# Scores of two attention pairs in one run each, and block sums spread by DMA instead of by the vector engine

## The chip, the cores and the metric

The kernel runs on one core of a Trainium2 chip. The metric is the device time of one execution in microseconds (us), lower is better. The engines are called PE (matrix), DVE (vector), ACT (scalar), POOL (GpSimd) and SP (SyncE). One more measure is taken from the traces and used below:

- **the middle stretch**: from the start of the second batch's routing logits (tile `lp`, at 67.20 us in the kernel before) to the start of the last group of eight matmuls (660.53 us). It leaves out the start of the program, which varies by a microsecond between executions, and the closing steps.

Ratios are computed as the mean time of one kernel's fast runs over that of the other's of the same rounds, so they are not quite the ratios of the medians that are quoted.

## The reference, cut to what matters

```python
# attention over (batch 4, heads 8, sequence 768, head dim 64): a band of +-15 positions
# plus 24 block summaries (maximum of keys, mean of values, blocks of 32)
scores_l = scale * q @ k.T                    # masked to |i - j| < 16
scores_s = scale * q @ k_sum.T + log(32)
out = softmax([scores_l, scores_s]) @ [v, v_sum]
# then a mixture of 8 experts on all 3072 rows, weighted by P
P = exp(x @ w_gate); 8 times: normalize the rows, then the columns
y = sum_e P[:, e] * (relu(x @ w1[e]) @ w2[e])
```

## The kernel before

Two heads make a *pair*: 16 pairs, four for each of four batches. While pairs are attended to, expert 0 is applied to the batches that are done; so the matrix engine always finds something to do. The order of instructions on every engine comes from a small planner in the program itself: each unit of work is given an engine, a planned cost and what it depends on, and the planner places the one that can start first. **A changed cost or dependency therefore moves other work too**, and each engine executes its work in the order placed, waiting where something is late (in one experiment below PE stood still for 6.6 us behind one late input). What follows are the parts that the change touches (cuts are marked with ...).

```python
    BY_DMA = 12
    X_BY_DMA = 12
    WHOLE = 12          # pairs from this one on: scores of all 6 chunks in one run
...
        def block_out(i):                 # block sums of the values, from PSUM, into chunk 0 of V_e
            ...
            nc.vector.tensor_tensor(out=dst..., in0=vs, in1=own_n..., op=ALU.mult)
            if i >= PB:                   # and from chunk 0 into chunks 1 to 5
                ve = V_e[i % NE]
                nc.vector.tensor_copy(out=ve[0:64, 1:G, :],
                                      in_=ve[0:64, 0:1, :].to_broadcast([64, G - 1, 2 * VD]))
...
        def scores(i):
            sg = at["sg", i, 0] = banks2("sg")                 # the one slot of two PSUM banks
            dst = [[sg[:, j, :] for j in range(2)], None]
            if i >= WHOLE:                                     # and two of the three small banks "a"
                dst[1] = at["sg", i, 1] = [bank("a", "sg1") for _ in range(2)]
            score_mms(i, dst, range(G if i >= WHOLE else HG))
...
        def score_mms(i, dst, chunks):
            for g in chunks:
                for j in range(2):        # the two heads: 64 rows each, two halves of the array
                    o = (g % HG) * LIVE
                    score_mm(i, dst[g // HG][j][:, o:o + LIVE], j, g, 0, LIVE)
...
                U["A", i, h] = add("PE", 0.4, lambda h=h: values(i, h),      # value products
                                   [U["mk", i, h], U["ed", i], U["sx", i, h], U["Vs", i], U["near", i]],
                                   prio, opens=[buf])
```

The softmax here doesn't subtract the row's maximum and nothing guards it: scores larger than these inputs give would overflow.

Of the kernel before, what the change touches and what calls it, by code (L numbers as in the profile page):

```python
# [33 lines left out]
class Plan:  # L34
# [7 lines left out]
    def add(self, eng, cost, fn, deps=(), prio=0.0, opens=(), uses=(), lag=0.0):  # L42
        u = Unit(eng, cost, fn, [d for d in deps if d is not None], prio, list(opens), lag)
        for b in list(opens) + list(uses):
            b.users.append(u)
        if uses and eng != "PE":
            u.prio -= 100.0
        self.units.append(u)
        return u
# [79 lines left out]
def kernel(  # L129
# [10 lines left out]
    nc = tc.nc  # L140

    B, H, S, D = q.shape
    G = S // 128
# [6 lines left out]
    NP = (B * H) // 2  # L150
    PB = H // 2
# [6 lines left out]
    VD = D + 1  # L158
    NEH = 3
    BY_DMA = 12  # L160
    X_BY_DMA = 12
    WHOLE = 12
    FILL = {"v0": 1, "S0": 1, "s0": 2, "s1": 1, "s2": 1}

    const = ctx.enter_context(tc.tile_pool(name="const", bufs=1))
# [56 lines left out]
    NE = 2  # L222
# [3 lines left out]
    with tc.manual_schedule():  # L226
# [12 lines left out]
        kT = [attn.tile([128, S], BF16, name=f"kT{i}") for i in range(NB)]  # L239
# [9 lines left out]
        V_e = [attn.tile([128, G, 2 * VD], BF16, name=f"Ve{i}") for i in range(NE)]  # L249
# [8 lines left out]
        add = plan.add  # L258
# [101 lines left out]
        def block_out(i):  # L360
            vs = at.pop(("vs", i))[0:64, :].rearrange("p (j d) -> p j d", j=2)
            dst = V_s[i][0:64, :] if i < PB else V_e[i % NE][0:64, 0, :]
            nc.vector.tensor_tensor(out=dst.rearrange("p (j x) -> p j x", j=2)[:, :, 0:D], in0=vs,
                                    in1=own_n[:].to_broadcast([64, 2, D]), op=ALU.mult)
            if i >= PB:
                ve = V_e[i % NE]
                nc.vector.tensor_copy(out=ve[0:64, 1:G, :],
                                      in_=ve[0:64, 0:1, :].to_broadcast([64, G - 1, 2 * VD]))


        def near_values(i):

# [9 lines left out]
        def scores(i):  # L382
            sg = at["sg", i, 0] = banks2("sg")
            dst = [[sg[:, j, :] for j in range(2)], None]
            if i >= WHOLE:
                dst[1] = at["sg", i, 1] = [bank("a", "sg1") for _ in range(2)]
            score_mms(i, dst, range(G if i >= WHOLE else HG))

# [232 lines left out]
        def wait_busy(what, i, h, t):  # L621
            for _ in range(FILL.get(what + str(i), 0) if i < PB and not h else 0):
# [6 lines left out]
                          in_=k[0, 0:2].rearrange("j (p g) d -> p j (g d)", g=G))  # L629
        nc.sync.dma_start(out=v_f32.rearrange("p j g d -> p (j g) d"),  # L630
                          in_=v[0, 0:2].rearrange("j (g p) d -> p (j g) d", p=128))
# [227 lines left out]
        U = {}  # L859
        last = [None, None]  # L860
# [20 lines left out]
        def pair_start(i, prio):  # L881
            o = i - NB
            war_k = [U.get(("S", o, 0)), U.get(("S", o, 1)), U.get(("km", o))]
            war_q = war_k[:2] + [U.get(("ss", o, 0)), U.get(("ss", o, 1))]
            ahead = U.get(("S", i - 1, 1 if i > PB else 0))
            if i >= BY_DMA:
                for z in range(2):
                    U["tr", i, z] = add("SP", 1.4, lambda z=z: tr_dma(i, z),
                                        [U["kq"[z], i], U.get(("S", i - 3, 1))] + (war_k, war_q)[z], prio)
                    U["kT", i, z] = add("DMA", 1.7, None, [U["tr", i, z]], prio, lag=2.0)  # L890
            for z in range(0 if i >= BY_DMA else 1 if i < PB else 2):
                buf = Buffer("m" if i < PB else "a")
                U["tr", i, z] = add("PE", 0.5 if i < PB else 0.34, lambda z=z: tr(i, z),
                                    [U["kq"[z], i], U["ident"]] + (war_k, war_q)[z]
                                    + [U["tr", i, 0] if z else ahead], prio, opens=[buf])
                U["kT", i, z] = add({"ACT": 0.8, "DVE": 0.95 if i < PB else 0.56}, 0,
                                    lambda z=z: tr_out(U["kT", i, z].on, i, z), [U["tr", i, z]], prio,
                                    uses=[buf])
            U["ks", i] = add("DVE", 0.95, lambda: key_max(i), [U["kT", i, 0], U.get(("km", o))], prio)
            if i >= PB:  # L900
                U["km", i] = add("DVE", 0.23, lambda: key_max_split(i), [U["ks", i]] + war_q[2:], prio)
            buf = Buffer("a")
            U["vs", i] = add("PE", 0.4, lambda: block_sums(i),
                             [U["v", i]] + ([U.get(("A", i - NE, 1)), U["vc", i % NE]] if i >= PB else []), prio + 0.01, opens=[buf])
            sc = add("DVE", 0.25, lambda: summary_constants(i), [], prio - 1.0) if 0 < i < PB else None
            U["Vs", i] = add("DVE", 0.28 if i < PB else 0.7, lambda: block_out(i), [U["vs", i], sc],
                             prio + 0.01, uses=[buf])

        def pair_half(i, h, prio):
# [34 lines left out]
        def pair_whole(i, prio):  # L944
            U["near", i] = add("SP" if i < BY_DMA else "POOL", 2.4 if i < BY_DMA else 3.0, lambda: near_values(i),
                               [U["v", i], U.get(("A", i - NE, 1)), U["vc", i % NE]], prio, lag=5.0 if i < BY_DMA else 3.5)
            x1 = []
            deps = [U["kT", i, 0], U["kT", i, 1], U.get(("ed", i - 2))]
            bufs = [Buffer("s")] + (2 * [None] if i < WHOLE else [Buffer("a"), Buffer("a")])
            U["S", i, 0] = U["S", i, 1] = add("PE", 0.4 if i < WHOLE else 0.6, lambda: scores(i), deps, prio,  # L950
                                              opens=[x for x in bufs if x is not None])
            U["X", i, 0] = add("ACT", 0.97, lambda: score_exp(i, 0), [U["S", i, 0]], prio, uses=bufs[:1])
            if i < WHOLE:
                buf = Buffer("s")
                U["S", i, 1] = add("PE", 0.4, lambda: scores_1(i), deps, prio, opens=[buf])
                U["X", i, 1] = add("ACT", 0.97, lambda: score_exp(i, 1), [U["S", i, 1], U["X", i, 0]], prio,
                                   uses=[buf])
            else:
                x1 = [add("ACT", 0.53, lambda j=j: score_exp(i, 1, j), [U["S", i, 0], U["X", i, 0]], prio,
                          uses=bufs[1 + j:2 + j]) for j in range(2)]  # L960
                U["X", i, 1] = x1[1]
            for h in range(2):
                U["mk", i, h] = add("DVE", 0.56, lambda h=h: masks(i, h),
                                    [U["X", i, h], *x1[:h], U.get(("A", i - 2, 1))], prio)
            U["ed", i] = add("DVE", 0.78, lambda: edges(i),
                             [U["X", i, 0], U["X", i, 1], U["mk", i, 1], U.get(("A", i - NE, 1)), U["ec", i % NE]], prio)
            buf = Buffer("a")
            U["ss", i, 0] = U["ss", i, 1] = add("PE", 0.22, lambda: summaries_2(i),
                                                [U["km", i], U["kT", i, 1], U.get(("A", i - NE, 1))], prio, opens=[buf])
            for h in range(2):  # L970
                U["sx", i, h] = add("ACT", 0.46, lambda h=h: summary_exp(i, h), [U["ss", i, h]], prio, uses=[buf])
            for h in range(2):
                buf = Buffer("a")
                U["A", i, h] = add("PE", 0.4, lambda h=h: values(i, h),
                                   [U["mk", i, h], U["ed", i], U["sx", i, h], U["Vs", i], U["near", i]],
                                   prio, opens=[buf])
                U["no", i, h] = add("DVE", 0.75, lambda h=h: normalize(i, h),
                                    [U["A", i, h], U.get(("x", i - 2))], prio, uses=[buf])
            if i >= X_BY_DMA and i % PB < PB - 1:
                U["xt", i] = add("SP", 1.5, lambda: x_dma(i), [U["no", i, 0], U["no", i, 1]], prio)  # L980
                U["x", i] = add("DMA", 1.7, None, [U["xt", i]], prio, lag=2.0)
                return
            buf = Buffer("a")
            U["xt", i] = add("PE", 0.35, lambda: to_xT(i), [U["no", i, 0], U["no", i, 1]], prio, opens=[buf])
            U["x", i] = add({"ACT": 0.8, "DVE": 0.55}, 0, lambda: x_out(U["x", i].on, i), [U["xt", i]], prio,
                            uses=[buf])
# [109 lines left out]
        def transposed():  # L1096
# [7 lines left out]
            for j in range(2):  # L1104
                nc.gpsimd.tensor_copy(out=warm[:, 2 + j:3 + j],
                                      in_=ve[64 + 32 * j:96 + 32 * j, G - 2, VD * j:VD * j + 1])

        last[0] = add("POOL", 0.3, transposed, [last[0], U["near", NP - 1]] + [U["kT", NP - 1, z] for z in range(2)]
                      + [U["x", i] for i in range(X_BY_DMA, NP - 1)])
        load("w1n", lambda: load_w1(1), 0.85, 5.0)  # L1110
        load("w2n", lambda: load_w2(1), 0.85, 5.0)
# [209 lines left out]
```

## Time and profile before

| | before |
|---|---|
| median of 6 runs | 666.79 us (666.71 to 667.56) |
| span of the profiled execution | 665.8 us |
| middle stretch, by the trace | 593.33 us |
| closing part, by the trace | 5.26 us |

The page's first part gives each engine's busy time and share of the span; 99% for PE says that it is the bound. A "busy" PE may still lose time between matmuls. That is read from the distance of successive start times in the timeline, compared with what their columns need, and the prediction below does so.

### The profile page before, as it was taken

To read this page: it belongs to the slowest core of one execution; us is meant where nothing else is said; L and a number is where in the kernel's file an instruction comes from. 1 tells how busy PE (TensorE), PEld (TensorE's weight loads), DVE (VectorE), ACT (ScalarE), POOL (GpSimd) and SP (SyncE) were. 2 spreads that over 40 slices of the span, in tenths; PEclk is the share of its full clock that TensorE was granted. 3 is DMA by queue.
4 is the path that set the end of the run, shared out by engine and by line. 5 is a ranking of instruction groups with operands and counts; after the bars stand their busy time and mean duration, and the time that the engine had idled before them with its cause. 6 is when DMAs were issued, how large, how long until landed. Compare 5 with 4: busy or idle time off the path is not lost.

```text
span 665.8 us, 13247 instructions
## 1 busy us (share of the span) xinstructions
PE 658.5 (99%) x5132; PEld 436.2 (66%) x5132; DVE 550.4 (83%) x1034; ACT 411.4 (62%) x769; POOL 198.8 (30%) x257
## 2 busy tenths in 40 slices
PE   9999999999999999999999999999999999999997
PEld 5666666555676666666666666666666666666666
DVE  7799977798989787887789887888778877988776
ACT  6667866556875566556565665656665656556652
POOL 8799722100132222222222222222122213222123
PEclk9999999999999999999999999999999999999999
DMA  9999992700763747473654756373837465334656
GB/s 166 163 142 146 124 107 42 127 0 1 129 118 58 126 74 116 79 127 64 105 96 66 131 80 110 65 127 64 128 64 131 72 100 96 64 64 110 156 135 202
DMA packets 112558, 67.89 MB, mean 102 GB/s; under 512 B 77936, under 2 KB 90480, under 8 KB 112496
## 3 DMA queue, kind: packets, MB, share of 16 engines
q0 software_dynamic: 94816, 57.46, 65.4%
q1 hardware_dynamic: 17152, 9.58, 6.8%
q8 instruction: 40, 0.66, 0.4%
q14 instruction: 22, 0.18, 0.1%
q10 hardware_dynamic: 528, 0.02, 0.0%
HBM read 52.45 MB, written 6.29 MB: 88 GB/s over the span
## 4 chain that ended last, share of the span: by engine, by line
PE 95%; DVE 2%; DMA 1%; POOL 1%; issue 0%; ACT 0%; POOLq 0%; DVEq 0%
PE yps L815 22%; PE pA L764 22%; PE pY L815 17%; PE pQ L764 11%; PE hps L211 6%; PE yps L216 6%; PE pR L764 5%; DMA w<-in_moe_w_dram 1%; PE sg L347 1%; PE tkq L303 1%; PE av L435 1%; PE av L512 1%; PE ss L461 1%; PE vs L357 1%; PE av L441 1%; PE tx L550 1%
## 5 line engine op out<-in xcount | busy, mean ns | idle before, releaser
L815 PEld LDWEIGHTS <-h 128*128 128x128 f16 x2352 | 230.1, 98 | 89.2 <-issue 1.3
L843 POOL DMA_DIRECT2D out_acc<-y x120 | 101.4, 888 | 372.4 <-ACT y L839 95.5
L839 ACT ACTIVATE y<-pY,P_sb 128x256 f32<-128x256 f32 x168 | 79.9, 476 | 126.3 <-PE pY L815 124.8
L830 DVE SCALAR_TENSOR_TENSOR out_acc<-yps,P_sb,out_acc 128x512 f32<-128x512 f32 x128 | 95.3, 745 | 28.0 <-PE yps L815 27.9
L798 DVE TENSOR_TENSOR h<-h 128x1024 f16<-128x1024 f16 x168 | 109.2, 684 | 1.3
L815 PE MATMUL pY<-w,h 128*128 128x256 f16 x672 | 100.3, 273 | 0.6 <-ACT y L839 0.6
L764 PE MATMUL pA<-xT,w 128*128 128x512 f16 x336 | 98.6, 379 | 0.0
L815 PE MATMUL yps<-w2sum,h 128*128 128x256 f16 x672 | 97.9, 273 | 0.0
L815 PE MATMUL yps<-w,h 128*128 128x256 f16 x672 | 93.3, 273 | 0.0
L830 DVE SCALAR_TENSOR_TENSOR out_acc<-pY,P_sb,out_acc 128x512 f32<-128x512 f32 x84 | 62.9, 749 | 29.1 <-PE pY L815 27.5
L764 PEld LDWEIGHTS <-w 128*128 128x128 f16 x672 | 65.8, 98 | 31.3 <-issue 0.2
L764 PEld LDWEIGHTS <-w1sum 128*128 128x128 f16 x504 | 49.3, 98 | 44.7
L786 DVE CUSTOM_DVE_ANT_0 h<-pQ,snap 128x512 f16<-128x512 f32 x84 | 57.7, 686 | 6.5 <-ACT snap L207 3.6
L786 DVE CUSTOM_DVE_ANT_0 h<-pA,snap 128x512 f16<-128x512 f32 x84 | 57.4, 684 | 5.4 <-PE pA L764 5.1
L202 ACT ACTIVATE h<-pA 128x512 f16<-128x512 f32 x84 | 50.7, 603 | 12.1 <-PE pA L764 12.0
L202 ACT ACTIVATE h<-pR 128x512 f16<-128x512 f32 x84 | 50.1, 596 | 8.1 <-PE pR L764 8.1
L207 ACT COPY pR<-pA 128x512 f32<-128x512 f32 x82 | 46.8, 571 | 6.8 <-PE pA L764 5.9
L815 PE MATMUL pY<-w2sum,h 128*128 128x256 f16 x336 | 50.4, 273 | 0.1
L764 PE MATMUL pA<-xsum,w 128*128 128x512 f16 x168 | 50.0, 379 | 0.0
L764 PE MATMUL pQ<-xsum,w1sum 128*128 128x512 f16 x168 | 50.0, 379 | 0.0
L764 PE MATMUL pQ<-xT,w1sum 128*128 128x512 f16 x168 | 50.0, 379 | 0.0
L764 PE MATMUL pA<-xsum,w1sum 128*128 128x512 f16 x168 | 50.0, 379 | 0.0
(150 smaller groups left out, 854.7 us busy)
## 6 DMA issues: line engine op xcount, KB each, us to landing
out_acc<-y POOLq DMA_DIRECT2D x120, 256.0 KB, 3.4
w<-in_moe_w_dram POOLq DMA_DIRECT2D x14, 1024.0 KB, 10.3
out_dram<-out_acc SPq DMA_DIRECT2D x24, 256.0 KB, 2.4
qst<-in_q_dram POOLq DMA_DIRECT2D x32, 96.0 KB, 5.8
vx<-in_v_dram POOLq DMA_DIRECT2D x15, 192.0 KB, 6.9
kst<-in_k_dram POOLq DMA_DIRECT2D x24, 96.0 KB, 6.1
w<-in_moe_w_dram POOLq DMA_DIRECT2D x4, 256.0 KB, 8.6
w<-in_moe_w_dram POOLq DMA_DIRECT2D x2, 512.0 KB, 8.8
```

What stands on the lines that cost most here:

```text
L202: nc.scalar.activation(out=out, in_=in_, func=AF.Relu, bias=0.0, scale=1.0)
L207: (nc.scalar.copy if eng == "ACT" else nc.vector.tensor_copy)(out=out, in_=in_)
L211: nc.tensor.matmul(hp[:, 0:n], lhsT=w1s[e][:, dk, f * 128:(f + 1) * 128], rhs=xT[:, dk, t0:t0 + n], start=(dk == 0), stop=(dk == KD - 1))
L216: nc.tensor.matmul(yp[:, d], lhsT=h[:, f, c * 128:(c + 1) * 128], rhs=w2s[e][:, f, d], start=(f == 0), stop=(f == KF - 1))
L303: nc.tensor.transpose(t[:, g * 128:(g + 1) * 128], st[:, g, :, :].rearrange("p j d -> p (j d)"), ident)
L764: nc.tensor.matmul(dst[:], lhsT=lhsT, rhs=rhs, start=first and k == 0, stop=k == HK - 1, skip_group_check=True)
L786: nc.vector._custom_dve(dve_ops.TENSOR_ADD_SAT, out=ring(e, p, q)[:, q % 2, blk, :], in0=at[src, e, p, q][:], in1=at.pop(("snap", n, e, p, ...
L798: nc.vector.tensor_tensor(out=h[:, :, out_, :], in0=h[:, :, a, :], in1=h[:, :, b, :], op=op)
L815: nc.tensor.matmul(dst[:, d], lhsT=lhsT, rhs=rhs, start=f == 0 and n in (1, 5, 2), stop=f == HF - 1, skip_group_check=True)
L830: nc.vector.scalar_tensor_tensor(out=o, in0=y, scalar=scalar, in1=o, op0=ALU.mult, op1=ALU.add)
L839: nc.scalar.activation(out=at[key][:, d], in_=src, func=AF.Copy, bias=0.0, scale=P_sb[:, t, e:e + 1])
L843: nc.gpsimd.dma_start(out=o, in_=at.pop(("y", e, p, c, key))[:], accum_op=ALU.add)
```

## The change

Its intent: a pair's scores in one run of 12 matmuls instead of two of 6 for two more pairs, and 1.9 us less work for DVE in the fourth batch, by letting DMA copy the block sums into the chunks.

```diff
-    WHOLE = 12
+    SPREAD = 12
+    WHOLE = 10
...
-            if i >= PB:
+            if PB <= i < SPREAD:
                 ve = V_e[i % NE]
                 nc.vector.tensor_copy(out=ve[0:64, 1:G, :], ...)
+        def spread_sums(i):
+            ve = V_e[i % NE]
+            nc.gpsimd.dma_start(
+                out=ve[0:64, 1:G, :], in_=ve[0:64, 0:1, :].to_broadcast([64, G - 1, 2 * VD]))
...
-            U["Vs", i] = add("DVE", 0.28 if i < PB else 0.7, lambda: block_out(i), ...)
+            U["Vs", i] = add("DVE", 0.7 if PB <= i < SPREAD else 0.28, lambda: block_out(i), ...)
...
+            if i >= SPREAD:
+                U["sp", i] = add("POOL", 1.0, lambda: spread_sums(i), [U["Vs", i]], prio, lag=3.5)
...
-                                   [U["mk", i, h], U["ed", i], U["sx", i, h], U["Vs", i], U["near", i]],
+                                   [U["mk", i, h], U["ed", i], U["sx", i, h], U.get(("sp", i), U["Vs", i]), U["near", i]],
...
-        last[0] = add("POOL", 0.3, transposed, [last[0], U["near", NP - 1]] + ...
+        last[0] = add("POOL", 0.3, transposed, [last[0], U["near", NP - 1], U.get(("sp", NP - 1))] + ...
```

More of the change, by code (lines that the diff above doesn't have):

```diff
@@ L905, in pair_start @@
             sc = add("DVE", 0.25, lambda: summary_constants(i), [], prio - 1.0) if 0 < i < PB else None
-            U["Vs", i] = add("DVE", 0.28 if i < PB else 0.7, lambda: block_out(i), [U["vs", i], sc],
+            U["Vs", i] = add("DVE", 0.7 if PB <= i < SPREAD else 0.28, lambda: block_out(i), [U["vs", i], sc],
                              prio + 0.01, uses=[buf])
@@ L1106, in transposed @@
                                       in_=ve[64 + 32 * j:96 + 32 * j, G - 2, VD * j:VD * j + 1])
-        last[0] = add("POOL", 0.3, transposed, [last[0], U["near", NP - 1]] + [U["kT", NP - 1, z] for z in range(2)]
+        last[0] = add("POOL", 0.3, transposed, [last[0], U["near", NP - 1], U.get(("sp", NP - 1))] + [U["kT", NP - 1, z] for z in range(2)]
                       + [U["x", i] for i in range(X_BY_DMA, NP - 1)])
```

## The prediction

> **What bounds the kernel now.** I read the page's first part, then the busy times by stretch, then the timeline where pairs 10 to 15 run. The first says that the matrix engine is the bound:
>
> ```profile
> PE 658.5 (99%) x5132; PEld 436.2 (66%) x5132; DVE 550.4 (83%) x1034; ACT 411.4 (62%) x769; POOL 198.8 (30%) x257
> ```
>
> A busy PE in this view can still lose time inside, so I compared the distance between the starts of successive matmuls with the time their columns need. The timeline gives that need: four 384-column matmuls start 0.65 us before what follows them, 0.163 us each, 2.36 columns a nanosecond. Where the change acts, the stretches read:
>
> ```profile
> 67.00:84.00 17.00, 16.95 (x203) 11.17 (x201) 15.94 (x45) 13.29 (x23) 11.71 (x15) 1.00 2.23 125
> 84.00:115.00 31.00, 31.00 (x302) 18.73 (x301) 24.14 (x68) 22.00 (x42) 8.43 (x18) 1.00 0.72 70
> 121.00:165.00 44.00, 44.00 (x234) 22.94 (x233) 39.98 (x86) 26.14 (x50) 0.00 (x0) 1.00 0.25 42
> 165.00:217.00 52.00, 51.87 (x363) 35.41 (x362) 47.85 (x76) 38.68 (x73) 12.67 (x15) 1.00 0.60 100
> 217.00:600.00 383.00, 383.00 (x2648) 258.93 (x2647) 313.87 (x484) 229.83 (x442) 87.93 (x104) 1.00 0.57 93
> ```
>
> The columns are length, then PE, weight loads, DVE, ACT and POOL busy. The matrix engine is full in all of them, because attention pairs and expert matmuls are interleaved: when a pair waits, an expert block runs. So an operation taken from another engine is worth nothing by itself; only a gap on PE, or less PE work, moves the end. Gaps of over 60 ns between matmuls add up to only about 2 us from 67 to 200 us, and to none from 200 to 600. That caps the gain near 2 us (0.3%).
>
> What are those gaps? Nearly all stand around the score matmuls, which contract over 64 rows and run as two halves of the array:
>
> ```profile
> 68.77 0.81 PE L211 MATMUL hps<-xT,w 128*128 128x384 f16 x4
> 69.52 0.38 PE L347 MATMUL sg<-qT,kT 64*128 64x160 bf16 x6
> 69.83 0.36 PE L435 MATMUL av<-vx,em 128*128 128x65 bf16 x6
> ...
> 93.19 0.81 PE L211 MATMUL hps<-xT,w 128*128 128x384 f16 x4
> 93.93 0.59 PE L347 MATMUL sg<-qT,kT 64*128 64x160 bf16 x12
> 94.45 2.76 PE L216 MATMUL yps<-w,h 128*128 128x512 f16 x12
> ```
>
> The run of 6 is the first half of pair 10. Four 384-column matmuls from 68.77 need 0.65 us, to 69.42, and the scores start at 69.52: 0.10 us lost on the way in. Six scores, two at a time, need 3 x 160 columns, 0.20 us, yet what follows starts 0.31 us later: 0.11 us lost on the way out. The run of 12 (pair 12, scored in one run already) loses the same: 93.93 - 93.19 - 0.65 = 0.09, and 94.45 - 93.93 - 0.40 = 0.12. **A run costs 0.2 us whatever its length.**
>
> **What the Trainium skill says.** "TensorEngine Tiling (Array Packing)", Key Properties: "Changing tiling mode (not just tile) drains the TensorE". The trace agrees, with 0.10 and 0.11 us at the edges of each 64-row run. "DMA: Bandwidth & Descriptors", Anatomy of one DMA, gives a fixed cost of about 2 us, mostly completion; the GpSimd-issued copies at 100 to 108 us land 1.7 to 2.9 us after issue, so it agrees when the queue is empty. While loads were still queued (issue at 83.7) the same copy took 10.8 us. That page, Issuing engines are not separate DMA queues, says that all issuers share the 16 DMA engines, which fits. How long the new, larger copy takes, no run shows yet.
>
> **The change part by part.**
>
> *Scores of pairs 10 and 11.* Each had two runs of 6 (69.52 and 71.30; 76.00 and 78.12) and gets one of 12. The columns stay; two runs vanish, 2 x 0.2 = **-0.4 us on PE**, on the path, as PE is the path. The price: the second half goes to two of the three small PSUM banks and needs two exponentials of 480 columns in place of one of 960. One of 960 lasts 0.97 us; the two of 480 of pair 15 start 0.45 us apart and together take 1.03, so ACT pays about 0.1 us a pair and has 3.7 us idle from 67 to 84. The banks are taken from transposes, sums and value products of neighbours; these may run later, but expert blocks fill in. I count 0 for it.
>
> *Block sums of pairs 12 to 15.* The vector engine's copy of one chunk into five goes:
>
> ```profile
> L367 DVE COPY Ve<-Ve x12: 483/483/485, 36.3 to 114.1; 64x650 bf16<-64x650 bf16 x12
> L377 POOL DMA_DIRECT2D Ve<-vx x8: 524/524/569, 83.7 to 107.1; - x8
> ```
>
> Four of the twelve copies, 4 x 0.48 = 1.9 us of DVE, between 84 and 115 us where DVE is idle 31.00 - 24.14 = 6.9 us: **0 on the path**. Added are four DMA issues on GpSimd, about 0.6 us each (its present ones take 0.52), where GpSimd is idle 22 us: 0 too. Landing: 64 x 5 = 320 packets of 260 bytes, 20 for each of 16 DMA engines; the page's queue line gives 65.4% x 16 x 665.8 us / 94816 = 73 ns a packet, so some 1.5 us on top of about 1.8: an estimate of 3 us. For pairs 12, 13 and 14 the sums end at 85, 92 and 101.5 us and their value products run at 98.5, 103.6 and 110.9, so a landing 3 us later, or as late as the queued copies that landed at 94 to 97, hides.
>
> **Pair 15 does not hide**, and this is where I hesitate:
>
> ```profile
> 113.83 0.28 DVE L363 TENSOR_TENSOR Ve<-vs,own_n 64x128 bf16<-64x128 f32 x1
> 114.14 0.48 DVE L367 COPY Ve<-Ve 64x650 bf16<-64x650 bf16 x1
> 115.39 0.35 PE L435 MATMUL av<-vx,em 128*128 128x65 bf16 x6
> ...
> 117.38 0.79 POOL L190 DMA_DIRECT2D w<-in_moe_w_dram  x1
> ...
> 120.71 0.35 DVE L579 TENSOR_REDUCE rs_sb<-P_sb 128x24 f32<-128x192 f32 x1 [1.56 <-ACT P_sb L574]
> ```
>
> Here the sums are the last input of the pair's value products. The program orders instructions by its own planned costs: the copy is planned at 0.7 us with the sums, the DMA at 0.28 + 0.15 + 1.0 + 3.5 and another hop. So the products will be placed 0.28 + 0.15 + 1.0 + 3.5 - 0.7 = 4.2 us later in PE's order, whatever the DMA really takes. All that hangs on them moves with them: the last transpose, the gate's logits, the weight load of the next expert (117.38) and the routing normalization (120.71). PE itself stays fed at that spot: from 115.39 to 127.9 it has the second half of the third batch's expert work, about 10 us, and 4.2 of it simply runs earlier.
>
> The bill may come later. From 121 to 165 us DVE is idle only 4.0 us of 44, and from 165 to 217 only 4.2 of 52: it works off routing, sums of x and of weights. The routing ends just as PE's filler does (the last L216 block is at 162.9, the first scaling that needs the routing at 163.69). Starting all this 4.2 us late leaves 8.2 us of idle DVE to catch up in, plus copies that the planner may hand to ACT (idle 17.9 and 13.3 us there). I take **0 to 2 us of new PE gaps, 0.3 as the likeliest**.
>
> *Sum.* 666.82 - 0.4 + 0.0 + 0.0 + 0.3 = 666.7; with the chance that nothing comes of the delay at all, I say **666.6 us**.
>
> **The rivals.**
> 1. *Pure gain*: the delay is swallowed whole; only the two drains count, perhaps a rearranged gap or two of 0.1 to 0.2 us more. For it: PE never waited for a pair after 67 us. It makes 666.0 to 666.4.
> 2. *The delay reaches PE*: after 165 us the filler is gone, the quads wait for DVE and the products for the routing weights. For it: DVE at 39.98 of 44 us. Against it: 8.2 us of slack and evacuations that may go to either engine. It makes 667.5 to 669.
> 3. *The DMA lands late and PE waits in order* at a value product of pair 12 or 13, behind the loads still in the queue. For it: landings of up to 10.8 us at 83.7. Against it: margins of 3 us and more, and the program plans 4.5 us. It makes 667 to 668.
> 4. *The copies were the bound*: DVE 1.9 us lighter makes all 1.9 us faster, 664.5. Against it: DVE has 6.9 us idle in that stretch and PE none.
>
> **Range and chances.** Rival 1 has some 45%, rival 2 about 30%, rival 3 about 10%, and small mixtures the rest. The three runs of before lie 0.8 us apart, which the range has to hold as well: 665.6 to 668.4. Two per cent are 13.3 us; nothing above comes near that, and removing every PE gap after 67 us gives 2. Within 2%: 0.985.
>
> **What would show it.** Right: sg runs of 12 for pairs 10 and 11, two runs fewer, each remaining one still losing 0.2 us; no L367 copies after 100 us; the added DMA landing in about 3 us; the first value product of pair 15 some 4 us after its sums with expert blocks in between; the routing starting near 125 us. PE gaps between 165 and 217 us decide between rivals 1 and 2. Wrong: value products of pairs 12 to 14 that wait for the new DMA, or a routing that starts no later than 121 us, which would mean that the sums of pair 15 were placed earlier. A change of over 2 us either way would mean that I mistook PE for full.

## The result

The changed kernel took **667.09 us** (median of 6, 666.75 to 668.23) against 666.79 us of before in the same rounds: ratio 1.0004, 95% interval 0.9991 to 1.0017. No difference is resolved. The page's first part, with the engines in the same order as before:

```profile
PE 656.6 (99%) x5131; PEld 436.0 (66%) x5132; DVE 547.5 (82%) x1030; ACT 411.0 (62%) x771; POOL 201.5 (30%) x261
```

DVE lost four instructions and POOL gained four, as the diff says. The busy times by stretch (length, then PE, weight loads, DVE, ACT, POOL; then granted clock, DMA share and GB/s):

```profile
67.00:84.00 17.00, 17.00 (x158) 10.77 (x156) 14.01 (x36) 10.69 (x21) 8.29 (x10) 1.00 2.30 130
84.00:115.00 31.00, 30.95 (x334) 19.29 (x333) 24.30 (x72) 23.25 (x44) 11.38 (x22) 1.00 0.36 67
165.00:217.00 52.00, 52.00 (x369) 35.82 (x367) 46.68 (x75) 39.93 (x75) 11.41 (x14) 1.00 0.64 106
```

PE is as full as it was, and from 165 to 217 us it even lost the 0.13 us of idle time that it had. From 67 to 84 us DVE, ACT and POOL do less than before: attention work has moved to later. The timeline of PE shows what moved, the scores of pair 10:

```profile
79.27 1.03 PE L217 MATMUL yps<-w,h 128*128 128x512 f16 x4
80.23 0.59 PE L348 MATMUL sg<-qT,kT 64*128 64x160 bf16 x12
80.75 0.51 PE L304 MATMUL tkq<-ident,kst 128*128 128x128 bf16 x6
```

It is one run of 12, as written, but at 80.2 us; before, the halves ran at 69.5 and 71.3. A run of 12 needs the double slot and two of the three small banks at once; by the program's text the planner can place it only when all of these are free, while a unit that needs one bank can go first. PE did expert blocks meanwhile. Then the copies and pair 15, in the tile view of the sums' copy and the timelines of POOL and PE:

```profile
L375 POOL DMA_DIRECT2D Ve<-Ve x4: 669/669/672, 90.3 to 106.2; - x4
...
DMA to landing us min/median/max: 2.3/2.5/3.2
```

```profile
105.42 0.28 DVE L364 TENSOR_TENSOR Ve<-vs,own_n 64x128 bf16<-64x128 f32 x1
...
106.25 0.67 POOL L375 DMA_DIRECT2D Ve<-Ve  x1
...
114.78 0.35 PE L442 MATMUL av<-vx,em 128*128 128x65 bf16 x6
...
120.75 0.35 DVE L586 TENSOR_REDUCE rs_sb<-P_sb 128x24 f32<-128x192 f32 x1 [2.21 <-ACT P_sb L581]
```

The sums of pair 15 are made at 105.4 us, not at 113.8, and its DMA lands 6 us before the value products at 114.8 want it. The routing starts at 120.75 us; before, at 120.71. The delay that the prediction feared did not take place.

**Where the time went** shows in the two measures. In the traces, the second logits and the last group of eight matmuls start at (before, then after):

```profile
67.20 0.74 PE L570 MATMUL lp<-wg_bf,xT 128*128 128x8 f16 x24
...
660.53 1.04 PE L815 MATMUL yps<-w,h 128*128 128x256 f16 x8
```

```profile
66.26 0.74 PE L577 MATMUL lp<-wg_bf,xT 128*128 128x8 f16 x24
...
658.98 1.04 PE L822 MATMUL yps<-w,h 128*128 128x256 f16 x8
```

The middle stretch fell from 593.33 to 592.71 us (658.98 - 66.26, with one more digit than printed): **0.62 us were won**. The closing part, from the start of the last group of eight matmuls to the end of the span, grew from 665.79 - 660.53 = 5.26 to 664.68 - 658.98 = 5.70 us: **0.44 us were given back** after the last matmul had begun. A gain of 0.18 us is left, less than the runs can resolve. (Second logits 0.94 us earlier is chance, as the first experiment shows.)

What stands in the closing part is POOL's closing drain, a `DRAIN` instruction that the profile puts on the last source line. In the view of that line, before and after, with durations in ns (least, median, most):

```profile
L1316 POOLq DRAIN  x3: 46/98/4910, 660.1 to 665.5; - x3
L1316 SPq DRAIN  x3: 7/7/13, 664.7 to 665.3; - x3
```

```profile
L1325 POOLq DRAIN  x3: 46/98/5357, 658.5 to 664.4; - x3
L1325 SPq DRAIN  x3: 7/7/13, 663.1 to 664.2; - x3
```

The first of POOL's three drains starts 1.2 us before the last matmul in both and lasts 4.91 and 5.36 us. It ends 3.70 and 4.15 us after that matmul's start; SP, which waits for the last output, is done after 3.43 us. So POOL ends last, and its 0.45 us are the 0.44 that the closing part grew by.

### The profile page after: what moved, and what is told of

It is laid out like the page before. It is cut to its first block, busy times and chain, and to the rows that moved or that the text cites. A ratio compares the mean times of both kernels' runs of the same rounds, so it can differ in the third digit from the quotient of the medians.

```text
span 664.7 us, 13262 instructions
## 1 busy us (share of the span) xinstructions
PE 656.6 (99%) x5131; PEld 436.0 (66%) x5132; DVE 547.5 (82%) x1030; ACT 411.0 (62%) x771; POOL 201.5 (30%) x261
## 3 DMA queue, kind: packets, MB, share of 16 engines
q0 software_dynamic: 95008, 57.79, 65.9%
## 4 chain that ended last, share of the span: by engine, by line
PE 95%; DVE 3%; DMA 1%; issue 0%; ACT 0%; SPq 0%; DVEq 0%
PE yps L822 22%; PE pA L771 22%; PE pY L822 17%; PE pQ L771 11%; PE hps L212 6%; PE yps L217 6%; PE pR L771 5%; PE sg L348 1%; DMA kvf<-in_v_dram 1%; PE av L519 1%; PE tkq L304 1%; PE vs L358 1%; PE av L442 1%; DVE xs L550 1%; PE ss L468 1%; PE av L448 1%
```

## The experiments

There are eleven runs, in three groups. Two of them are the kernels before and after, run again. The medians of the kernel before in the rounds of each group were 667.68, 667.08 and 666.83 us. The middle stretch and the closing part are read from each run's trace as above; two profiles of one kernel agree in the middle stretch to 0.01 us (below), so that it resolves what the times cannot. It serves as long as the second logits themselves don't move, which they do in the last two runs (0.7 us later and 1.3 us earlier). The expectations count to the start of the single last matmul, which is 0.76 us after the group's, so their stretches are 0.76 us longer.

| kernel | median us | ratio to before (95%) | middle stretch | closing part |
|---|---|---|---|---|
| before, again | 667.12 | 0.9990 (0.9975 to 1.0005) | 593.33 | 5.26 |
| changed, again | 667.12 | 0.9992 (0.9977 to 1.0006) | 592.71 | 5.70 |
| scores alone | 666.74 | 0.9984 (0.9970 to 0.9999) | 592.61 | 5.25 |
| sums by DMA alone | 667.65 | 0.9997 (0.9982 to 1.0013) | 593.40 | 5.71 |
| 30 more mode switches | 674.26 | 1.0103 (1.0086 to 1.0121) | 599.47 | 5.71 |
| the same 30 matmuls, no switch | 667.75 | 1.0009 (0.9993 to 1.0025) | 593.35 | 5.70 |
| pair 15 late | 667.53 | 1.0008 (0.9990 to 1.0025) | 593.86 | 5.71 |
| sums' copies from SP | 666.50 | 1.0001 (0.9970 to 1.0033) | 592.71 | 5.25 |
| scores alone, no small copies on POOL | 665.68 | 0.9985 (0.9971 to 0.9998) | 592.61 | 4.98 |
| sums of pairs 8 to 11 by DMA too | 675.26 | 1.0133 (1.0119 to 1.0148) | 600.65 | 5.91 |
| pairs 8 and 9 in one run too | 670.37 | 1.0060 (1.0046 to 1.0073) | 597.34 | 5.70 |

### The noise: both kernels once more

No edit. Expected of the kernel before:

> The kernel before, once more, against itself: the noise of this comparison. Theory A (two drains of the matrix engine are saved, little else matters): ratio 1.000, and a second profile of it shows whether the 0.9 us by which the first one lagged at 40 us (same instructions in the same order there) was chance in the landing of a weight load. Theory B (the change makes everything before 67 us faster): the second profile lags again by 0.9 us.

and of the changed one:

> The changed kernel, once more. Theory A: 0.2 to 0.6 us faster than before, ratio about 0.9993, since matmul gaps of over 60 ns after 67 us fell by 0.56 us in its profile. Theory B (what is won between 67 and 217 us is given back at the end or in small gaps): ratio 1.000 to 1.001, as in the first result (1.0004), and the distance from the second routing logits to the last matmul no shorter than in the kernel before.

Both took 667.12 us. Their middle stretches repeat: 593.33 twice for before, 592.71 twice for the change. The second profile of the kernel before has its second logits at 66.23 us, as early as the changed kernel: the 0.94 us in the first profile came from two loads that landed late (there, PE's waits of the first 25 us have 0.4 us for values, `vx`, and 0.3 us for an expert weight, `w`; in the second profile they have neither), so theory B of the first text falls. Theory A of the second holds for the stretch and is wrong for the whole; theory B is right that something is given back, and right that it is at the end, but not that the distance to the last matmul is no shorter.

### Each part alone

```diff
-    SPREAD = 12            # scores alone: no pair is spread by DMA
+    SPREAD = 16
```

> Only the scores of pairs 10 and 11 in one run; the vector engine still spreads the sums. Theory A (the drains are the whole effect): same time and same gaps as the changed kernel, pair 10 scored near 80 us as there. Theory C (the late scores of pair 10, 80 us and not 70, come from the spread): pair 10 scored near 70 us and the time differs from the changed kernel's by 0.3 us or more.

The scores alone won 593.33 - 592.61 = **0.72 us** in the middle and nothing was lost at the end; 0.9984 is the first ratio whose interval lies below 1, but the kernel before got 0.9990 against itself in the same rounds, so it is the trace that shows the gain and not the time. Pair 10 was scored at 80.3 us here too, so the late scores come from this part. The 0.72 us can be counted in the trace: gaps over 60 ns (from one matmul's start to the next, less what its columns need at the prediction's 2.36 a nanosecond) from the second to the fourth logits sum to 1.52 us before and 1.13 here, 0.39 less: two runs fewer. Another 0.29 us was a gap at 180 us in the kernel before, whose cause the profile doesn't name:

```profile
179.77 1.32 PE L815 MATMUL pY<-w2sum,h 128*128 128x256 f16 x8
180.93 0.60 PE L815 MATMUL pY<-w,h 128*128 128x256 f16 x4
```

Eight such matmuls need 8 x 0.109 = 0.87 us, but the next group starts 1.16 us later. Neither this kernel nor the changed one has such a gap between the fourth logits and 217 us. That part is luck of the new order, not the idea.

```diff
-    WHOLE = 10             # sums by DMA alone: pairs 10 and 11 in two runs as before
+    WHOLE = 12
```

> Only the spread of the sums by DMA; pairs 10 and 11 in two runs each. Theory A: the time of before within 0.2 us, 0.4 us more gaps than the changed kernel. My forecast's step for pair 15: its sums stay at 112 us, its value products go to 119 to 120 us, the routing starts near 125, and 0 to 2 us are lost. Against it: its sums are placed early as in the changed kernel (105 us), nothing is delayed.

The sums' part alone **lost 0.07 us** in the middle and 0.45 at the end. Nothing was won by taking 1.9 us off DVE. The step of the forecast for pair 15 is refuted here as well: its sums ran at 105.35 us (matmuls of `vs`) and its value products at 113.6, earlier than before, and the last logits at 117.5. What had held the sums back to 112.5 in the kernel before was their place in the order: behind the scores of pair 15, at 107.0, and the value products of pair 14, all of which draw on the same three small banks (`sg` are the scores of pair 15, `vs` the matmuls of its sums; before, then with the sums' part alone):

```profile
106.99 0.59 PE L347 MATMUL sg<-qT,kT 64*128 64x160 bf16 x12
...
112.46 0.50 PE L357 MATMUL vs<-vx,m_blk 128*128 128x128 bf16 x6
```

```profile
105.35 0.50 PE L358 MATMUL vs<-vx,m_blk 128*128 128x128 bf16 x6
...
107.08 0.59 PE L348 MATMUL sg<-qT,kT 64*128 64x160 bf16 x12
```

In this kernel and in the changed one the planner placed the sums ahead of those scores. Which of its planned numbers tips this was not tested.

### What one switch of the array's mode costs

```diff
                     score_mm(i, dst[g // HG][j][:, o:o + LIVE], j, g, 0, LIVE)
+                if i >= WHOLE and g < G - 1:
+                    nc.tensor.matmul(dst[g // HG][0][:, 480:512], lhsT=zeros[0:128, 0:128], rhs=zeros[0:128, 0:32],
+                                     start=True, stop=True)
```

and for the control `zeros[0:64, ...]` in both operands. The results of the kernel don't change, as the columns are not read.

> The changed kernel, and in each of the six score runs of pairs 10 to 15 five matmuls of 128 rows by 32 columns on zeros, into unused columns of the score bank: 30 more switches out of the two-halves mode and back. The program's planned costs and so all orders are untouched. Theory A (each switch pair drains the matrix engine for 0.2 us, and the engine is full, so it all reaches the end): 30 x 0.21 + 30 x 0.013 = 6.7 us slower from the second routing logits to the last matmul. Rival (gaps on the engine are absorbed by waits elsewhere): under 2 us.

> The control of the run with added switches: the same 30 matmuls with 64 rows, so without a change of mode. Theory A: 0.4 to 0.9 us slower (30 times 13 to 30 ns). If it is the added matmuls as such and not the mode: as slow as the other, near 6.7 us.

With switches, the middle stretch grew by 599.465 - 592.712 = **6.75 us**, expected 6.7; without, by 593.346 - 592.712 = 0.63. So a switch out of the two-halves mode and back costs (6.75 - 0.63) / 30 = **0.204 us**, the load of the 128-row weights that comes with it included, and all of it reached the end: no gap on PE is absorbed here. The timeline shows it; two score matmuls side by side need 160 columns, 0.07 us, and here:

```profile
80.57 0.24 PE L348 MATMUL sg<-qT,kT 64*128 64x160 bf16 x2
80.74 0.19 PE L406 MATMUL sg<-zeros 128*128 128x32 bf16 x1
80.87 0.24 PE L348 MATMUL sg<-qT,kT 64*128 64x160 bf16 x2
```

From one pair of scores to the next it is 0.30 us. In the time of the runs it is 674.26 against 667.75 us.

### The delay that did not happen, made on purpose

```diff
-                U["sp", i] = add("POOL", 1.0, lambda: spread_sums(i), [U["Vs", i]], prio, lag=3.5)
+                U["sp", i] = add("POOL", 1.0, lambda: spread_sums(i), [U["Vs", i]], prio,
+                                 lag=11.5 if i == NP - 1 else 3.5)
```

> The delay that my forecast feared, made on purpose: the changed kernel with the planned landing of pair 15's sums 8 us later, so that its value products, the last logits and the routing are placed later (planned: products 4.7 us, routing weights 6.5 us later). Forecast's rival 2: 0.9 to 2.5 us slower than the changed kernel, as gaps or fewer matmuls between 165 and 217 us. Its rival 1 (swallowed whole): within 0.2 us.

The value products of pair 15 came at 119.3 us, 4.5 us later than in the changed kernel, and the middle stretch is **1.14 us** longer (593.86 - 592.71). PE's gaps over 60 ns from the fourth logits to 217 us grew from 0.87 to 2.02 us, which is that 1.14; the largest is 0.73 us at 181 us, and 0.34 us came at 153 us, earlier than rival 2 had it. The view of PE's waits from 165 to 217 us has one line where the kernel before has none:

```profile
PE yps L822 <- DVE out_acc L837: 0.6, 1, 0.6
```

So rival 2 of the forecast is a real mechanism of the size that was named (0.9 to 2.5 us); it merely was not set off.

### Where the end was lost

```diff
         def spread_sums(i):
-            nc.gpsimd.dma_start(
+            nc.sync.dma_start(
```

> The changed kernel with the four copies of the sums issued from SyncE's queue; planned order untouched. Theory D (GpSimd's closing drain, which grew from 4.91 to 5.36 us with the four copies, is the 0.45 us by which the tail after the last matmul grew): the drain is back at 4.91, the tail at 4.49, and the kernel 0.45 us faster than the changed one. Rival (the tail grew for another reason, such as the other program size): tail stays 4.94.

The same four copies, issued from SP: the drain is back, and with it the closing part (5.25 us), while the middle stretch stays at 592.71.

```profile
L1325 POOLq DRAIN  x3: 46/98/4910, 658.5 to 663.9; - x3
```

The four copies on POOL's queue, 550 us earlier, cost 0.45 us at the end of the program. The median, 666.50 us, is 0.6 below that of before, but this kernel's mean was spoilt by one run of 670.57, so its ratio says nothing; the trace decides.

```diff
-    SPREAD = 12
+    SPREAD = 16
...
-            eng = nc.sync if i < BY_DMA else nc.gpsimd      # near_values: 16 copies of 10 KB
+            eng = nc.sync
```

> Scores of pairs 10 and 11 in one run, sums spread by the vector engine, and the 16 small copies of neighbouring values of pairs 12 to 15 issued from SyncE instead of GpSimd; planned orders untouched. If GpSimd's closing drain grows with the number of copies it issued (0.45 us for 4, 0.11 each), it falls by 1.8 us to 3.1; if with their packets (1280 here, 1280 in the four copies of the sums), by 0.45 to 4.46; if with neither, it stays 4.91. In the first two cases SyncE's own end, 3.43 us after the last matmul, sets the tail: 4.2 us and not 4.49. The stretch from second logits to last matmul as with the scores alone (593.37) unless SyncE's queue makes the copies late. If all that holds it is the fastest yet: 1.0 us below the kernel before.

```profile
L1325 POOLq DRAIN  x3: 45/102/4580, 658.3 to 663.5; - x3
```

The drain shrank by 0.33 us: not the 1.8 of "so much a copy", nor quite the 0.45 of the second case. What that case calls packets are contiguous runs (16 x 80 here, 4 x 320 there). In the profile POOL's queue has 512 packets fewer here and has 192 more with the four copies, so "so much a packet" would have been 1.2 us, and that fails as well. Now POOL is done 3.37 us after the last matmul's start and SP's 3.43 sets the end; the closing part is 4.98 us. Together with the scores, this version takes (593.33 + 5.26) - (592.61 + 4.98) = **1.0 us** less than the kernel before by the trace, as expected. It is the fastest of all: 665.68 us, ratio 0.9985 (0.9971 to 0.9998).

### The same two ideas, taken further

```diff
-    SPREAD = 12            # and alone, in the other kernel: WHOLE = 8
+    SPREAD = 8
```

> The changed kernel with the sums of pairs 8 to 11 spread from GpSimd's queue too, where that queue is full of loads. By copies or packets GpSimd's drain grows by another 0.45 us to 5.81 and the tail to 5.39. My forecast's rival 3 (late landings, the matrix engine waits in order): landings of 5 to 10 us against the planned 4.5, some of the value products of pairs 8 to 11 wait, 0.5 us or more of new gaps before 100 us. If its landings hide there too: no new gap, only the tail.

Rival 3 of the forecast, at full size. POOL works through its instructions in order, and in this part of the program it is issuing loads:

```profile
58.39 0.28 DVE L364 TENSOR_TENSOR Ve<-vs,own_n 64x128 bf16<-64x128 f32 x1
```

```profile
69.44 1.64 POOL L285 DMA_DIRECT2D qst<-in_q_dram  x2 [0.19 <-issue]
71.06 1.44 POOL L375 DMA_DIRECT2D Ve<-Ve  x2
```

```profile
PE av L448 <- DMA Ve<-Ve: 6.6, 1, 6.6
```

The sums of pair 8 were ready at 58.7 us, POOL issued their copy at 71.1, it landed 8.7 us later, and PE stood for 6.6 us. The wait cost more than its length, as the granted clock was lower after it. The stretch from 80 to 85 us has it in the column before the last two, as 0.62:

```profile
80.00:85.00 5.00, 5.00 (x49) 3.64 (x47) 3.42 (x10) 0.59 (x2) 4.21 (x5) 0.62 0.96 67
```

Four 384-column matmuls start 0.32 us apart at 80.6 us, where 0.163 is usual. Together with what the slower ones lost, the middle stretch is 7.94 us longer than in the changed kernel. The drain was 5.28 us, not the 5.81 expected, so it doesn't grow steadily with the copies either; the closing part was 5.91 us, with a later pause of POOL in it that I can't explain.

> The changed kernel with pairs 8 and 9 scored in one run too. By switches alone 0.4 us less than the changed kernel (593.08 from second logits to last matmul). Rival: a run of 12 needs two of the three shared banks at once and is placed late; the plan has the last logits 2.7 us later than in the changed kernel and its own end 4.8 us later, so that the matrix engine runs out of expert blocks: 1 us or more slower.

The switches saved are worth 0.4 us, yet the kernel took 670.37 us, 3.5 more than before. The scores of pairs 8 to 15 come 1 to 9 us later than in the changed kernel, the last logits at 122.4 us, and PE has 2.3 us of gaps over 60 ns from 165 to 217 us, where the changed kernel has none: at the same place as with the delayed pair 15, so probably by the same mechanism, which no run isolates here. From 60 us to the second logits there are 1.54 us of gaps (changed kernel: 0.59), where the new order waits mostly for DVE at the end of the second batch. The second logits came 1.3 us earlier in this order, so the middle stretch of the table, 4.63 us longer, overstates the loss: the last group of matmuls starts 3.3 us later.

## Why the prediction was right, and where it was wrong

The time, 667.09 us, lies in the range (665.6 to 668.4), 0.5 above the 666.6 named, and "within 2%" was right. That says little: the range is 2.8 us wide and would have held no change as well. By the trace the net gain, 0.18 us, is close to the 0.2 named, but that is luck, as three errors nearly cancelled: 0.3 us for pair 15 that was not lost, 0.29 us from a gap that vanished, and 0.45 us at the end that nobody had counted. Its parts fared differently.

- **PE is the bound, work taken from other engines is worth nothing: right.** DVE lost 1.9 us of copies in the fourth batch, and the kernel with that part alone got 0.07 us slower in the middle. Rival 4 is out.
- **"Gaps of over 60 ns ... add up to only about 2 us", "nearly all" around the scores: the cap held, the count was off.** By the count used here the kernel before has 1.52 + 1.15 = 2.7 us from the second logits to 217 us. The 1.52 stand around scores; of the rest, 0.87 stand behind eight small `sink` matmuls and 0.29 is the gap at 180 us.
- **A run costs 0.2 us whatever its length, two fewer give 0.4 us on PE: right, and shown.** 0.204 us for a switch and back by 30 added ones; 0.39 us fewer gaps where two runs vanished.
- **Other users of the banks may run later, counted as 0: right in its value.** Pair 10 was scored 11 us later and expert blocks filled the time. Two more pairs, and it was no longer 0 but some 3 us.
- **The copies for pairs 12 to 14 hide: right, and the estimate of 3 us partly by luck.** Landing was 2.3 to 3.2 us, issue 0.67 for 0.6. But the 320 packets a copy of the estimate were not there: POOL's queue went from 94816 to 95008 packets, 48 a copy, of 4160, 1040 and 4 bytes, so sixteen runs of 260 bytes travel in one packet. Issued from SP, the same copy made 336.
- **"The products will be placed 0.28 + 0.15 + 1.0 + 3.5 - 0.7 = 4.2 us later in PE's order": wrong.** The step took the planner's place for the sums of pair 15, 112.5 us, as given, and moved only what follows. The sums moved as well, to 104.7 us, and the DMA had time to spare. So the 0.3 us that the sum took for it was 0; an enforced delay of 4.5 us cost 1.14.
- **A term was missing.** "Added are four DMA issues on GpSimd ..., where GpSimd is idle 22 us: 0 too" looked only at the issue. POOL's closing drain, 0.45 us longer for these copies, is on the path that sets the end.
- **0.29 us came from a gap that the new order removed**, and whose cause stays open; it is of the kind that rival 1 had as "perhaps a rearranged gap or two".

The middle is told to 0.1 us: -0.39 for the switches, -0.29 for the gap at 180 us, and +0.12 for a longer gap at 97.3 us between the scores and value products which the changed kernel has and the scores alone have not, -0.56 in all, of 0.62 measured. With +0.44 at the end, what is left is -0.18 us. The runs don't contradict it and can't confirm it.

What stays open: what POOL does in its closing drain and what sets its length, and why the planner moved the sums.

## What to carry to other kernels

Where one engine is full, count what it loses at the edges of its own work (here 0.2 us for each visit to another array mode) and not what other engines do; and expect that merging visits pays only while the larger demand on buffers doesn't push dependent work behind the last filler. When an order is made by a planner, a changed cost can move the operation's inputs too, so read their new place before adding delays. Look at the closing instructions as well: on this program four DMAs on GpSimd's queue in the first sixth of the run cost about 0.1 us where they stood and 0.45 us at the end.

## What the Trainium skill lacked or had wrong

- "TensorEngine Tiling (Array Packing)", Key Properties: says that a change of tiling mode drains the matrix engine, but not what it costs. Here it is 0.204 us for a switch from 128 rows to 64 and back (30 added switches, 6.75 us, less 0.63 for the matmuls as such).
- "DMA: Bandwidth & Descriptors" has nothing of the price that DMAs issued from GpSimd have at the end of a program. Its closing drain took 4.91 us before, 5.36 with four more copies of 64 x 5 runs, 5.28 with eight more, 4.58 without 16 small ones, and 4.91 when the four came from SyncE.
- The same page, Anatomy of one DMA, gives some 2 us of fixed cost. The copies of the sums landed in 2.3 to 3.2 us with a free queue; behind queued loads one took 8.7 us, after a further 12 us until GpSimd came to issue it. The page has no figure for a DMA behind queued loads, which is what an operation that others wait for needs.
